# Reordering filter placement, back tables and filler in the prologue of a fused FFT filter and ReGLU kernel

## The chip, the cores and the metric

The kernel runs on one core of a Trainium2 chip. A core has TensorE (PE) for matmuls, VectorE (DVE), ScalarE (ACT) and GpSimd (POOL) for elementwise work, and SyncE (SP), which here only issues DMAs. Each engine runs its instructions in its program order and waits on semaphores of the others. The metric is the device time of one execution in microseconds (us).

## The reference

For x of shape (8, 3008, 256) the reference filters each of the 256 columns along the sequence in the frequency domain, and sends every one of the 24064 resulting rows through a gated feed-forward layer:

```python
X = np.fft.rfft(x, axis=1)
F = (filt_r + 1j * filt_i)[None, :, :]     # (1505, 256)
y = np.fft.irfft(X * F, n=3008, axis=1)    # (8, 3008, 256)

x = y.reshape(24064, 256)
gate = np.maximum(x @ w_gate, 0.0)         # (256, 1536)
val = x @ w_val                            # (256, 1536)
out = (gate * val) @ w_out                 # (1536, 256)
```

## The kernel before

**The transform.** 3008 is 94 x 32, and the transform of a batch is done in two steps by matmuls. `items_a` multiplies x by the table `WA` (94 points) and writes the result to DRAM (`Abuf`); `load_at` reads it back into the tile `at` in another order. Then come six groups i = 0 to 5, in `first_b` for batch 0: `fwd` (line 364) multiplies `at` by the table `F2` (32 points) into two PSUM tiles `psX`, one for each e = 0, 1; `product` (lines 377 to 380) multiplies each `psX` by the filter, `tt` with the real part `Ftr` and `uu` with the imaginary part `Fti`; and `inv` (line 394) multiplies `tt` by the back table `I2t` and `uu` by the back table `I2u`, and adds both in PSUM (`psD`). ScalarE copies `psD` to `dsb`, which goes to DRAM (`Dbuf`) and is read back as `dC`. `item_c` applies the last table `M1` and gives `yT`.

**The layer.** `gv` and `o_part` do the feed-forward layer in 47 blocks of 512 rows, with 12 steps each. The transforms of batches 1 to 7 are placed between these steps at written positions. This steady part begins with the first `item_c`, after the prologue.

**The prologue.** The schedule is manual: on each engine the instructions stand in the order in which the program calls them. The prologue transforms batch 0 and prepares, in this order:

- x is loaded by SP. GpSimd's queue loads the filters (lines 220 and 223: four large loads for `Ftr`, then four for `Fti`; then lines 228 and 231, for each filter a small load of 16 KB into groups 22 and 23 of rows 64 to 95, and one row `nyq`).
- `warm(11)` is filler: matmuls on a constant tile whose result nobody reads (`psJ`, line 511). Then follow the 16 transforms of `items_a(0)`.
- `make_back_t(i)`, three times: matmuls that permute `F2` (line 192), and two VectorE copies into `I2t` (line 197). `make_back_u(i)`, three times: a matmul of `I2t` with a table (line 202), and a ScalarE copy into `I2u` (line 203). After each of the six steps stands `warm(6)`, and one more at the end.
- `place_filter(fi, a, half, copy)` (line 238) copies one half of the 24 groups of a filter (fi 0 is `Ftr`, 1 is `Fti`) from 32 partitions to the next 32; a chooses partitions 0 to 63 or 64 to 127. The four copies for `Ftr` stand between `make_back_t` and `make_back_u`, those for `Fti` behind `place_own` (lines 209 and 211: tables of the last groups, and `M1`). `place_nyq` (line 242) is last.
- Then `first_b(amid)`. Its order on TensorE is fwd 0, filler, fwd 1, filler, fwd 2, inv 0, transforms of batch 1, fwd 3, inv 1, and so on. `amid(0)` and `amid(1)` are filler of 256 columns, the later ones take one or two transforms of `items_a(1)`.

In `product`, a pair (i, e) that is in `POOL_U` has its `uu` made by GpSimd: ScalarE first copies `psX` to `xs` (line 377), since GpSimd reads no PSUM here, and GpSimd multiplies (line 378). All else is made by VectorE (line 380). The two readers of one `psX` follow one another: `xs` is copied when `tt` is done.

## Time and profile before

| | |
|---|---|
| median of 4 runs | 905.04 us (904.13 to 907.09) |
| the profiled execution's own time | 904.13 us |
| its span, first to last instruction | 902.3 us |
| mean granted TensorE clock | 0.993 |
| busy: TensorE, VectorE, ScalarE, GpSimd | 878.6, 568.7, 502.3, 359.4 us |
| first product `psX` of batch 0 on TensorE | starts at 36.22 us |
| first filter product on VectorE | starts at 38.04 us |
| first matmul of the steady part (line 451) | starts at 62.97 us |

All times inside the execution count from the start of the span. A timeline row gives start, length, engine, line, operation, output and inputs and the count, and in brackets how long the engine had been idle before it, and what ended that. A DMA issue row ends with the microseconds from issue to landing. In a table of stretches, the busy time of each engine stands with the number of its instructions, and the last three columns are the granted TensorE clock as a share of full clock, the busy share of the DMA engines, and GB/s. The recorded ends of matmuls are modelled.

### The profile page before, as it was taken

The page shows a single profiled execution, that of the slowest core. Times are in us where ns is not written, and L with a number is a line of the kernel's source. Part 1 is how long each engine was busy: PE and PEld are TensorE (multiplying, and loading weights), DVE is VectorE, ACT ScalarE, POOL GpSimd, SP SyncE. Part 2 cuts the span into 40 slices and gives each one's busy share as a digit, 9 for nine tenths or more (in the row PEclk, how much of TensorE's full clock was granted, in tenths as well). Part 3 has the DMA queues.
Part 4 walks back from the last instruction along what each step waited for, and adds up shares of the span by engine and source line. Part 5 has one row for each costly group of instructions (what it writes and reads, how often), then busy time and mean ns, then how long its engine had stood idle before and what let it go on. Part 6 is the DMA issues. An engine that isn't in the chain of part 4 may idle for free.

```text
span 902.3 us, 19072 instructions
## 1 busy us (share of the span) xinstructions
PE 878.6 (97%) x7089; PEld 511.7 (57%) x7210; DVE 568.7 (63%) x872; ACT 502.3 (56%) x891; POOL 359.4 (40%) x352
## 2 busy tenths in 40 slices
PE   7899999999999999999999999999999999999997
PEld 2335555566555565566655666555655566666664
DVE  2637766577765776667766677657766577655553
ACT  3475565555655555555665565655565555555552
POOL 4232299228670486515773167801868000000000
PEclk9999999999999999999999999999999999999999
DMA  8979358534465344553364433763346512331111
GB/s 233 307 180 192 99 148 192 113 81 112 138 151 123 97 129 124 140 131 109 96 174 122 109 100 104 182 129 85 111 141 148 119 30 82 83 70 36 37 33 50
DMA packets 113759, 109.18 MB, mean 121 GB/s; under 512 B 20290, under 2 KB 98370, under 8 KB 113026
## 3 DMA queue, kind: packets, MB, share of 16 engines
q1 hardware_dynamic: 90662, 80.40, 34.8%
q0 software_dynamic: 22176, 26.01, 12.0%
q10 hardware_dynamic: 828, 1.54, 0.5%
q8 instruction: 57, 0.93, 0.4%
q14 instruction: 36, 0.29, 0.1%
HBM read 61.93 MB, written 49.81 MB: 124 GB/s over the span
## 4 chain that ended last, share of the span: by engine, by line
PE 80%; POOL 5%; DVE 4%; DMA 4%; ACT 4%; issue 3%; SPq 0%; DVEq 0%; POOLq 0%
PE psG L467 24%; PE psO L486 23%; PE psV L467 22%; DVE prod L472 3%; PE psF L323 3%; ACT vsb L470 3%; PE psD L394 2%; PE psA L276 2%; PE psX L364 2%; PE psY L451 1%; DMA WgT<-in_moe_w_gate_dram 1%; DMA XP<-in_x_dram 1%; POOL XP L296 1%; PE psJ L511 1%; DMA XF<-in_x_dram 1%
## 5 line engine op out<-in xcount | busy, mean ns | idle before, releaser
L472 DVE SCALAR_TENSOR_TENSOR prod<-psG,vsb 128x512 bf16<-128x512 f32 x564 | 389.3, 690 | 265.6 <-ACT vsb L470 256.4
L470 ACT CAST vsb<-psV 128x512 bf16<-128x512 f32 x564 | 332.1, 589 | 267.5 <-PE psV L467 203.6
L486 PE MATMUL psO<-WoT,prod 128*128 128x256 bf16 x2256 | 336.5, 273 | 1.1
L467 PE MATMUL psG<-yT,WgT 128*128 128x512 bf16 x1107 | 330.8, 379 | 6.9 <-ACT dsb L401 0.6
L467 PE MATMUL psV<-yT,WvT 128*128 128x512 bf16 x1030 | 315.3, 380 | 1.2 <-ACT yT L456 1.2
L486 PEld LDWEIGHTS <-prod 128*128 128x128 bf16 x2256 | 220.6, 98 | 143.4
L467 PEld LDWEIGHTS <-WgT 128*128 128x128 bf16 x1128 | 109.9, 98 | 136.2 <-issue 2.2
L467 PEld LDWEIGHTS <-WvT 128*128 128x128 bf16 x1128 | 98.4, 98 | 42.3 <-issue 30.9
L258 POOL CAST scr<-yT 128x8 f32<-128x8 bf16 x25 | 4.8, 191 | 266.2 <-ACT yT L456 266.2
L492 ACT COPY osb<-psO 128x512 f32<-128x512 f32 x92 | 54.0, 586 | 27.4 <-PE psO L486 26.3
L380 DVE TENSOR_TENSOR tt<-psX,Ftr 128x512 bf16<-128x512 f32 x96 | 65.1, 683 | 5.1 <-PE psX L364 5.0
L309 POOL TENSOR_TENSOR fold<-XP 128x1024 f32<-128x1024 f32 x24 | 56.6, 2356 | 21.9 <-PE psF L323 20.7
L380 DVE TENSOR_TENSOR uu<-psX,Fti 128x512 bf16<-128x512 f32 x89 | 60.6, 681 | 0.0
L401 ACT CAST dsb<-psD 128x512 bf16<-128x512 f32 x96 | 51.5, 589 | 13.0 <-PE psD L394 12.8
L310 POOL TENSOR_TENSOR XP<-XP 128x1024 f32<-128x1024 f32 x24 | 56.4, 2350 | 1.9
L296 POOL DMA_DIRECT2D XP<-in_x_dram x96 | 56.4, 592 | 0.9 <-issue 0.5
L330 DVE CAST asb<-psF 128x512 bf16<-128x512 f32 x48 | 30.9, 686 | 19.3 <-PE psF L323 15.0
L330 ACT CAST asb<-psF 128x512 bf16<-128x512 f32 x48 | 25.8, 589 | 29.0 <-PE psF L323 29.0
L456 ACT CAST yT<-psY 128x512 bf16<-128x512 f32 x47 | 27.6, 586 | 24.8 <-PE psY L451 24.2
L458 DVE CAST yT<-psY 128x512 bf16<-128x512 f32 x47 | 32.0, 681 | 10.8 <-PE psY L451 10.8
L451 PE MATMUL psY<-M,dC 96*128 96x94 bf16 (+18 forms) x604 | 37.5, 198 | 0.1
L451 PEld LDWEIGHTS <-dC 96*128 96x128 bf16 x604 | 34.5, 97 | 3.5 <-issue 1.2
(66 smaller groups left out, 479.8 us busy)
## 6 DMA issues: line engine op xcount, KB each, us to landing
at<-Abuf SPq DMA_DIRECT2D x32, 384.0 KB
dC<-Dbuf SPq DMA_DIRECT2D x64, 192.0 KB
XP<-in_x_dram POOLq DMA_DIRECT2D x48, 256.0 KB, 6.0
Dbuf<-dsb SPq DMA_DIRECT2D x23, 512.0 KB
XP<-in_x_dram POOLq DMA_DIRECT2D x96, 96.0 KB, 2.7
Abuf<-asb SPq DMA_DIRECT2D x96, 96.0 KB
out_dram<-osb SPq DMA_DIRECT2D x70, 94.0 KB
XF<-in_x_dram SPq DMA_DIRECT2D x15, 256.0 KB
```

Source lines behind the costliest of these rows:

```text
L296: nc.gpsimd.dma_start(xp[r:r + 24, 0:4:2, :], _ap(x, (b * N1 * N2 + o) * D, [[N2 * D, 24], [47 * N2 * D, 2], [1, 512]]))
L309: tt(t, xp[:, 0:2], xp[:, 2:4], op=ALU.add)
L310: tt(xp[:, 2:4], xp[:, 0:2], xp[:, 2:4], op=ALU.subtract)
L330: copy(asf[:, :, q, :], banks[q])
L380: nc.vector.tensor_tensor(p, psX, filt, op=ALU.mult)
L401: nc.scalar.copy(dsb[:, a, o:o + 2, :], psD[a])
L451: nc.tensor.matmul(psY[:, o:o + w], dCs[b, n2 // 8][:, n2 % 8, h * 128:(h + 1) * 128], M1[:, n1:n1 + w], start=True, stop=True)
L467: nc.tensor.matmul(pt[:, :W], w[:, h, ft * 128:(ft + 1) * 128], yt[:, h, :], start=(h == 0), stop=(h == 1))
L470: nc.scalar.copy(vsb, psV[:, :W])
L472: nc.vector.scalar_tensor_tensor(prod, in0=psG[:, :W], scalar=0.0, in1=vsb, op0=ALU.max, op1=ALU.mult)
L486: nc.tensor.matmul(psO[:, t % 2], prods[ft][:, t * 128:(t + 1) * 128], WoT[:, ft, :], start=(ft == 0), stop=(ft == NFT - 1))
L492: copy(osb[:, t0 % 2:t % 2 + 1], psO[:, t0 % 2:t % 2 + 1])
```

## The change

The order of the prologue's preparation is rewritten. The four placements of `Ftr` come first, ahead of the back tables. The three `make_back_t` follow one another, and then the three `make_back_u`, with no filler between them. Of `Fti`, the first placement (a = 0, first half, on VectorE) and the second (a = 1, first half, now on ScalarE) stand ahead of `place_own`, the two of the second half behind it, both on VectorE; before, ScalarE had a = 0 of the second half. All seven `warm(6)` stand at the end. In `POOL_U` the pair (0, 0) is replaced by (1, 0): the first pair has both its products on VectorE, and (1, 0) has its `uu` on GpSimd. `amid(0)` and `amid(1)` issue 5 filler matmuls instead of 3.

```diff
-    POOL_U = ((0, 0), (0, 1), (1, 1), (2, 0), (2, 1), (3, 1), (4, 0))
+    POOL_U = ((0, 1), (1, 0), (1, 1), (2, 0), (2, 1), (3, 1), (4, 0))
...
-    for i in range(3):
-        make_back_t(i)
-        warm(6)
     for half in range(2):
         for a in range(2):
             place_filter(0, a, half, nc.vector.tensor_copy)
     for i in range(3):
+        make_back_t(i)
+    for i in range(3):
         make_back_u(i)
+    place_filter(1, 0, 0, nc.vector.tensor_copy)
+    place_filter(1, 1, 0, nc.scalar.copy)
+    place_own()
+    place_filter(1, 0, 1, nc.vector.tensor_copy)
+    place_filter(1, 1, 1, nc.vector.tensor_copy)
+    place_nyq()
+    for i in range(7):
         warm(6)
-    warm(6)
-    place_own()
-    for half in range(2):
-        for a in range(2):
-            place_filter(1, a, half, nc.vector.tensor_copy if a or not half else nc.scalar.copy)
-    place_nyq()
     load_x(1, nc.sync, ((0, 0, 2 * q), (0, 2 * q, 4 * q), (1, 0, 4 * q)))
 
     early = items_a(1)
 
     def amid(i):
         if i < 2:
-            warm(3, 256)
+            warm(5, 256)
         else:
             for _ in range((1, 1, 2, 1, 1)[i - 2]):
                 next(early)()
```

## The prediction

> **What bounds the kernel now.** I read the page first, then the waits of TensorE, then the timeline of the first 66 us engine by engine, then the DMA issues with their landings, and last the granted clock in stretches of 3.41 us.

> The page's first part: span, then busy time, share and instructions by engine.

> ```profile
> span 902.3 us, 19072 instructions
> PE 878.6 (97%) x7089; PEld 511.7 (57%) x7210; DVE 568.7 (63%) x872; ACT 502.3 (56%) x891; POOL 359.4 (40%) x352
> ```

> TensorE is the bound. The waits of TensorE from 66 us to the end (total, times, longest) start like this:

> ```profile
> PE psG L467 <- ACT dsb L401: 0.6, 1, 0.6
> PE psG L467 <- DVE prod L472: 0.5, 2, 0.3
> PE psG L467 <- DMA WgT<-in_moe_w_gate_dram: 0.4, 1, 0.4
> ```

> Behind the prologue there is almost no wait in which a delay could vanish. So the end moves by what the prologue's last inverse product moves, one for one. Here is the stretch that the change rearranges, from the timeline (start, duration, what, idle before):

> ```profile
> 25.36 0.35 PE L192 MATMUL psI<-tabs,F 64*64 64x64 bf16 x16
> 29.09 0.76 DVE L197 CAST I2t<-psI 128x256 bf16<-128x256 f32 x2 [0.92 <-PE psI L192]
> 29.88 3.87 DVE L238 COPY Ftr<-Ftr 32x3072 bf16<-32x3072 bf16 x4
> 33.54 2.75 PE L511 MATMUL psJ<-junk 128*128 128x512 bf16 x12
> 36.22 0.41 PE L364 MATMUL psX<-at,F 64*64 64x256 bf16 x8
> 38.04 1.89 DVE L380 TENSOR_TENSOR tt<-psX,Ftr 128x512 bf16<-128x512 f32 x3
> 38.77 1.18 ACT L377 COPY xs<-psX 128x512 f32<-128x512 f32 x2 [1.67 <-DVE tt L380]
> 39.44 3.54 POOL L378 TENSOR_TENSOR uu<-xs,Fti 128x512 bf16<-128x512 f32 x3 [2.57 <-ACT xs L377]
> 41.75 0.42 PE L394 MATMUL psD<-uu,I2u 64*64 64x256 bf16 x3 [0.75 <-POOL uu L378]
> ```

> Two things are to be seen. TensorE has no gap from 25.36 to 38.18, because filler lies between the table steps. And its first forward product is ready long before VectorE, which placed filters until 38.01; from 38.18 TensorE mostly waits, until GpSimd's second product ends at 41.71.

> The DMA issue that turns out to decide the change (size, us from issue to landing), and where GpSimd issued it:

> ```profile
> Ftr<-in_filt_r_dram POOLq DMA_DIRECT2D x1, 16.0 KB, 15.1
> 13.34 0.57 POOL L228 DMA_DIRECT2D Ftr<-in_filt_r_dram x1
> ```

> Issued at 13.34, it lands at 13.34 + 15.1 = 28.45. Last the clock (stretch, length, PE busy, ..., the last three PEclk, DMA share, GB/s):

> ```profile
> 9.91:13.32 3.41, 1.06 (x4) 0.23 (x3) 0.00 (x0) 1.16 (x2) 3.41 (x7) 1.00 0.86 243
> 13.32:16.73 3.41, 3.41 (x5) 1.13 (x6) 0.00 (x0) 0.58 (x1) 0.59 (x2) 0.50 1.11 248
> 37.21:40.62 3.41, 1.57 (x23) 0.67 (x16) 3.35 (x8) 1.17 (x2) 1.19 (x2) 1.00 0.98 334
> 40.62:44.04 3.42, 2.66 (x14) 0.91 (x13) 1.70 (x3) 2.04 (x5) 2.23 (x2) 0.50 0.98 317
> 61.10:64.52 3.42, 2.49 (x17) 1.13 (x16) 0.69 (x1) 2.38 (x5) 0.00 (x0) 1.00 0.98 153
> ```

> A stretch with 1.06 or 1.57 us of TensorE work is followed by half clock; 2.49 us is not. The half clock ended after 3.4 us once (13.32) and after 6.8 us once (40.62), where the first stretch held only 2.66 us of work.

> **Part 1: Ftr's four placements go ahead of the back tables.** Each takes 0.95 us (row 29.88). Nothing is added; the order on VectorE changes. The fourth one (second half, rows 64 to 95) reads what line 228 loads, since groups 22 and 23 of those rows are in it. Before, it ran at 32.8 and the load had landed. Now it stands at the head of VectorE's queue at 24.3 and waits for 28.45. Behind it on VectorE are the six copies of the back tables; for them waits TensorE (line 202), and behind that stands all the filler. The first three placements are hidden: their loads have landed by 22.4, where GpSimd's waits for the Ftr loads end. GpSimd's nyq issue at 22.45 shares that moment; even if it slipped by the two copies, 1.9 us, its landing at 28.95 would come before line 242 needs it.

> Worked out: the fourth placement runs 28.5 to 29.45; three pairs of table copies at 0.76 (row 29.09, less overlap) end at 30.2, 30.9 and 31.6; the three matmuls of line 202 follow each pair, the last at 31.65, and filler starts at 31.95. Meanwhile the three steps of line 192, 0.28 each, are done at 26.2. TensorE is idle from 26.2 to 30.25, 4.05 us, then works 0.2 in each 0.7.

> **Part 2: all 42 filler matmuls behind.** Their number stays; six took 1.29 in the chain, so they need 7 x 1.3 = 9.1 us at full clock. In the old order they filled the waits of part 1, and the first forward product started at 36.22. Now that cover is gone. At full clock they end at 31.95 + 9.1 = 41.05. But the idle stretch is emptier than either that lost the clock, so I take half clock. It returns 3.4 to 6.8 us after filler starts, which costs half of that, 1.7 to 3.4. With this trace's 3.41 us grid (the next edges after 33.80 are 37.21 and 40.62) the first full stretch ends at 37.21: 5.26 us at half clock, 2.63 lost. First forward product: 43.68 instead of 36.22, between 41.05 (no loss) and 44.4.

> [...] The trace shows a fall after a gap of only 2.3 us (10.87 to 13.22), so the rows decide.

> **Part 3: Fti's placements, own tables, nyq.** One of the four stays on ScalarE (2.75 us), three on VectorE (0.95 each), own and M1 copies 0.2 each. After 31.6 they need 0.95 + 0.8 + 1.9 + 0.4, so VectorE ends at about 35.6 and ScalarE at 32.8 + 2.75 = 35.55. This is 2.4 us sooner than 38.01, and worth nothing, as the forward product comes at 43.68. The data of that product (at, landed by 34.65) are not last either.

> **Part 4: which product goes to GpSimd.** Seven before, seven after; (0,0) becomes VectorE's, (1,0) GpSimd's. Before, from the first tt to the end of the last product that the first inverse needs: 41.71 - 38.04 = 3.67. After: two tt/uu at the 0.60 pace, tt 0.69, step 0.07, ScalarE's copy 0.59, step 0.08, GpSimd 1.16: 3.79, a loss of 0.12. GpSimd then has four more in a row that the second and third inverse need, 4 x 1.15 = 4.6; ScalarE's copies for them are hidden behind GpSimd. Before, its chain broke at 43.0 to 44.23 and the cold TensorE ended later.

> **Part 5: 5 instead of 3 filler matmuls, twice.** Four more at 0.107 are 0.43 us. They lie in the wait before the first inverse; uncovered they would cost 0.43. TensorE is through its third forward product 2.15 us after its first starts, at 45.8, and then waits for 47.9 with some 0.5 of tt work in it.

> No DMA issue is moved or added on SP, ScalarE or GpSimd; at and the next x keep their clock times, and all that uses them runs later.

> **The sum.** The first product reads its matmul 0.45 after that starts (row pair 47.68, 48.13): 44.13. The first inverse's last operand: 44.13 + 3.79 = 47.92, against 41.71. Does the clock fall there again? The stretch 44.04 to 47.45 holds 1.75 + 0.5 = 2.25 us of work; 1.57 lost it and 2.49 kept it, and 2.25 is nearer to 2.49, so no. Then TensorE is quick and GpSimd is last: 47.92 + 4.6 = 52.5 for the third inverse, whose tail is 0.3; the next transform starts at 52.8 instead of 48.46. That is **+4.3 us**. What follows in the prologue (transforms, Dbuf's way to dC, weights) is released by that chain and moves with it. The profiled execution took 904.13 (span 902.3 and 1.83 around it), the fastest of four; it would be 908.4. Against the median of 905.04: 909.3.

> **The rivals.**

> A, as summed: with the half clock lasting 3.4 to 6.8 us the first forward product lies at 42.75 to 44.4, so 908.3 to 910.1.

> B, the clock falls in the product gap too: the first inverse's tail is at 47.95 instead of 41.75, with the same slow stretch behind it, +6.2: 911.2. For it: a stretch's edges may lie otherwise. Against: the gap of 3.57 becomes 2.1.

> C, the other side: the 16 KB load is not late. If it lands by 24.7, table copies start at 25.73, filler at 28.3, the forward product at 37.4, GpSimd's third-inverse operand at 37.4 + 0.45 + 3.79 + 4.6 = 46.24, the next transform at 46.55 against 48.46: -1.9, 903.1. The point of balance is a forward product at 39.3. That is 12.6 behind the landing at full clock, so a landing at 26.7, or 25.0 with the least clock loss: 1.7 to 3.4 us sooner than shown. For it: the queue's landings can vary. Against: Fti's last large load, ahead of it in the queue, lands at 12.75 + 15.5 = 28.25.

> E, the block comes but TensorE's clock holds: forward product at 41.05, 3.65 later than in C, +1.75: 906.8. Against: two emptier-than-half stretches lost it.

> **How the numbers follow.** A 0.50, B 0.23, C 0.15, E 0.09, still later 0.03. About 0.2% (1.8 us) is what a measurement can tell from no change. C gives most of "faster" (0.11) and the rest of "same" with half of E (0.08); all else is slower (0.81). The range 906.6 to 912.0 holds A, B and E and leaves out C and the late rest; A alone is 908.3 to 910.1.

> **What would show it.** Right: VectorE idle before a line 238 copy until about 28.5, released by Ftr's DMA; TensorE idle near 26 to 30; PEclk 0.5 for 3 to 7 us in the filler; the first line 364 at 43 to 44; VectorE's placements done by 36. Wrong: no DMA wait on VectorE, or the first line 364 before 39.3 (C), filler at full clock (E), or PEclk 0.5 again behind the first inverse (B).

## The result, and the profile after

| | before | after |
|---|---|---|
| median | 905.88 us (60 runs, 901.55 to 910.75) | 909.34 us (39 runs, 905.21 to 917.39) |
| ratio | | 1.0038, 95% interval 1.0027 to 1.0049 |
| profiled execution, its span | 904.13, 902.3 us | 911.06, 909.3 us |
| first forward product, line 364 | 36.22 us | 42.03 us |
| transform behind the third inverse, line 276 | 48.46 us | 51.63 us |
| first matmul of the steady part, line 451 | 62.97 us | 66.14 us |

The changed kernel is slower by 0.38%: 3.5 us by the medians, between 2.4 and 4.4 by the interval. The median forecast was 909.3.

The timeline of the changed kernel, VectorE and TensorE, in the stretch that the change rearranged (start, duration, what, idle before and what ended it):

```profile
22.09 1.92 DVE L238 COPY Ftr<-Ftr 32x3072 bf16<-32x3072 bf16 x2 [4.49 <-DMA Ftr<-in_filt_r_dram]
28.54 0.95 DVE L238 COPY Ftr<-Ftr 32x3072 bf16<-32x3072 bf16 x1 [4.52 <-DMA Ftr<-in_filt_r_dram]
29.52 2.08 DVE L197 CAST I2t<-psI 128x256 bf16<-128x256 f32 x6
...
24.14 0.74 PE L192 MATMUL psI<-tabs,F 64*64 64x64 bf16 x48
30.33 1.91 PE L202 MATMUL psI<-I2t,tabs 128*128 128x512 bf16 x3 [5.45 <-DVE I2t L197]
32.03 0.63 PE L511 MATMUL psJ<-junk 128*128 128x512 bf16 x1
32.89 9.21 PE L511 MATMUL psJ<-junk 128*128 128x512 bf16 x40 [0.22 <-issue]
42.03 0.41 PE L364 MATMUL psX<-at,F 64*64 64x256 bf16 x8
46.27 0.30 PE L394 MATMUL psD<-uu,I2u 64*64 64x256 bf16 x3 [0.94 <-POOL uu L378]
51.63 1.96 PE L276 MATMUL psA<-XF,WA 128*96 128x512 f32 x4
```

Of the two waits on line 238, the first, 4.49 us, is harmless: nothing waits for VectorE yet. The second, 4.52 us, is the fourth placement of Ftr. It starts at 28.54, directly behind the landing of the small load, whose issue row (size, us to landing) in the same trace is:

```profile
Ftr<-in_filt_r_dram POOLq DMA_DIRECT2D x1, 16.0 KB, 15.8
...
12.63 0.57 POOL L228 DMA_DIRECT2D Ftr<-in_filt_r_dram  x1
```

12.63 + 15.8 is 28.43. Behind that placement come the table copies at 29.52, for which TensorE has waited 5.45 us; the filler that used to lie in this wait follows it and ends only at 42.1.

The clock, in stretches of 3.41 us (stretch, length, busy time of PE, PEld, DVE, ACT and POOL with counts; the last three are PEclk, DMA share, GB/s):

```profile
23.47:26.88 3.41, 1.41 (x50) 0.63 (x48) 0.54 (x1) 1.08 (x2) 0.00 (x0) 1.00 1.14 270
26.88:30.30 3.42, 0.00 (x0) 0.00 (x0) 1.73 (x4) 0.00 (x0) 0.00 (x0) 0.50 1.10 342
30.30:33.71 3.41, 3.05 (x6) 0.93 (x8) 3.23 (x9) 2.58 (x4) 0.00 (x0) 0.50 0.67 210
33.71:37.12 3.41, 3.41 (x17) 1.57 (x16) 1.85 (x4) 1.92 (x1) 2.25 (x3) 1.00 1.00 315
43.95:47.36 3.41, 2.12 (x28) 0.95 (x26) 2.80 (x5) 2.33 (x5) 2.29 (x3) 1.00 0.82 146
```

The granted clock fell from 1.00 to 0.50 at 26.88, while TensorE was still idle, and returned at 33.71. So only the first 1.7 us of filler, from 32.03 on, ran at half clock. In the wait before the first inverse (43.95 to 47.36) it held, at 1.00.

Last, the longest waits of TensorE from 66 us to the end (total, times, longest):

```profile
PE psG L467 <- DMA WgT<-in_moe_w_gate_dram: 1.5, 1, 1.5
PE psX L364 <- issue: 1.4, 1, 1.4
PE psV L467 <- ACT yT L456: 1.2, 1, 1.2
```

The first two were 0.4 and 0.4 before; the third also stood in the trace of before, at 64.78, just outside that view. The profiled spans differ by 7.0 us, of which the prologue holds 3.17. By the first output copy (line 492) the difference is 5.27, and behind the ninth it is 6.66. Such waits change from run to run in all kernels of this study: in the nine traces the wait for WgT was between 0 and 1.5 us, that of line 364 between 0 and 1.6. From the ninth to the tenth output copy it took 10.6 to 13.1 us, in no order that follows the edits (10.6 in "old products" below, which has the loss, and 13.1 in "products alone", which has not). From line 451 to the first output copy, however, the two kernels with the loss are the longest: 24.9 us in after and 24.5 in "old products", against 22.7 to 23.6 in the seven others. With one trace of each kernel it stays open whether a part of the loss arises there.

The medians differ by 3.5, close to the prologue's 3.17. But 3.17 compares one pair of executions, and x came 1.2 us earlier in that of after (the table matmuls of line 192 start at 24.14 against 25.36). In after the load is waited for and not x. The order of before follows x: in "products alone" the table matmuls start 0.49 earlier than in before and the first line 364 0.48 earlier. So beside an equally early x the prologue's step would be nearer 4.4 (an estimate: 3.17 + 1.2).

### The profile page after: what moved, and what is told of

It is laid out like the page before. It is cut to its first block, busy times and chain, and to the rows that moved or that the text cites. A ratio compares the mean times of both kernels' runs of the same rounds, so it can differ in the third digit from the quotient of the medians.

```text
span 909.3 us, 19080 instructions
## 1 busy us (share of the span) xinstructions
PE 877.4 (96%) x7094; PEld 511.1 (56%) x7214; DVE 568.7 (63%) x872; ACT 502.1 (55%) x891; POOL 360.4 (40%) x352
## 4 chain that ended last, share of the span: by engine, by line
PE 77%; POOL 5%; DMA 5%; DVE 4%; ACT 4%; issue 4%; SPq 0%; POOLq 0%; DVEq 0%; ACTq 0%
PE psG L467 23%; PE psO L486 23%; PE psV L467 22%; DVE prod L472 3%; ACT vsb L470 3%; PE psF L323 3%; PE psD L394 2%; DMA Ftr<-in_filt_r_dram 2%; PE psX L364 1%; DMA WgT<-in_moe_w_gate_dram 1%; PE psY L451 1%; DMA XP<-in_x_dram 1%; PE psJ L511 1%; POOL XP L296 1%; POOL fold L309 1%
## 5 line engine op out<-in xcount | busy, mean ns | idle before, releaser
L472 DVE SCALAR_TENSOR_TENSOR prod<-psG,vsb 128x512 bf16<-128x512 f32 x564 | 389.3, 690 | 267.0 <-ACT vsb L470 259.0
L467 PE MATMUL psG<-yT,WgT 128*128 128x512 bf16 x1107 | 330.7, 379 | 8.2 <-DMA WgT<-in_moe_w_gate_dram 1.5
L467 PE MATMUL psV<-yT,WvT 128*128 128x512 bf16 x1030 | 315.3, 380 | 1.2 <-ACT yT L456 1.2
L467 PEld LDWEIGHTS <-WgT 128*128 128x128 bf16 x1128 | 109.8, 97 | 137.6 <-issue 2.3
L467 PEld LDWEIGHTS <-WvT 128*128 128x128 bf16 x1128 | 98.4, 98 | 42.3 <-issue 30.9
L380 DVE TENSOR_TENSOR tt<-psX,Ftr 128x512 bf16<-128x512 f32 x96 | 65.1, 683 | 11.6 <-PE psX L364 11.6
L380 DVE TENSOR_TENSOR uu<-psX,Fti 128x512 bf16<-128x512 f32 x89 | 60.6, 681 | 0.0
L401 ACT CAST dsb<-psD 128x512 bf16<-128x512 f32 x96 | 51.5, 589 | 12.1 <-PE psD L394 11.7
L330 DVE CAST asb<-psF 128x512 bf16<-128x512 f32 x48 | 30.9, 686 | 20.5 <-PE psF L323 18.3
L330 ACT CAST asb<-psF 128x512 bf16<-128x512 f32 x48 | 25.8, 589 | 30.4 <-PE psF L323 30.4
```

What stands on the lines that cost most here:

```text
L330: copy(asf[:, :, q, :], banks[q])
L380: nc.vector.tensor_tensor(p, psX, filt, op=ALU.mult)
L401: nc.scalar.copy(dsb[:, a, o:o + 2, :], psD[a])
L467: nc.tensor.matmul(pt[:, :W], w[:, h, ft * 128:(ft + 1) * 128], yt[:, h, :], start=(h == 0), stop=(h == 1))
L472: nc.vector.scalar_tensor_tensor(prod, in0=psG[:, :W], scalar=0.0, in1=vsb, op0=ALU.max, op1=ALU.mult)
```

## The experiments

The theory: the fourth placement of Ftr waits on VectorE for the small load; the table copies, TensorE's table matmuls and all filler stand behind it, and the cover that filler gave is gone. The rivals: the product part costs the time; or filler at the end costs by its place alone; or the load is not what is waited for.

In the table, "tables" is the start of line 192 on TensorE, which depends on when x arrives and differs from run to run; "gap" is from there to the first line 364. The gap shrinks by itself when x comes late and the load is no longer so far behind it, so it is compared with care.

| kernel | tables | line 364 | gap | line 451 | median | ratio to before, 95% interval |
|---|---|---|---|---|---|---|
| before | 25.36 | 36.22 | 10.9 | 62.97 | 905.88 | |
| after | 24.14 | 42.03 | 17.9 | 66.14 | 909.34 | 1.0038 (1.0027 to 1.0049) |
| fourth placement behind | 27.26 | 39.15 | 11.9 | 63.26 | 903.25 | 0.9977 (0.9955 to 0.9998) |
| small load early | 24.97 | 36.98 | 12.0 | 61.09 | 904.81 | 0.9989 (0.9969 to 1.0009) |
| filler between | 25.06 | 37.79 | 12.7 | 63.69 | 904.54 | 0.9993 (0.9970 to 1.0016) |
| old products | 26.37 | 40.69 | 14.3 | 66.94 | 909.48 | 1.0035 (1.0014 to 1.0056) |
| products alone | 24.87 | 35.74 | 10.9 | 61.72 | 905.08 | 0.9998 (0.9971 to 1.0025) |
| early load, 30 filler | 26.95 | 36.43 | 9.5 | 60.54 | 902.99 | 0.9972 (0.9952 to 0.9993) |
| early load, 18 filler | 27.08 | 35.97 | 8.9 | 60.08 | 902.44 | 0.9969 (0.9950 to 0.9988) |

The first four experiments and the last three were run on two different chips. The runs of before beside the first four had a median of 905.92, beside the last three 904.95, so kernels of the two groups are compared by their ratios.

**The fourth placement behind the table copies.** One instruction of the changed kernel moves:

```diff
     for half in range(2):
-        for a in range(2):
+        for a in range(2 - half):
             place_filter(0, a, half, nc.vector.tensor_copy)
     for i in range(3):
         make_back_t(i)
+    place_filter(0, 1, 1, nc.vector.tensor_copy)
     for i in range(3):
         make_back_u(i)
```

> The changed kernel, with only its fourth placement of Ftr (the one that reads the 16 KB load) moved behind the three make_back_t. Theory (the wait for the small load holds VectorE, and with it table copies, TensorE and all filler): the table copies start at about 24.4 instead of 29.5, filler at 27, the first line 364 at about 36.0 instead of 42.0, with no stretch of half clock in the filler; the transform behind the third inverse at about 45.6 instead of 51.6. Time 6 us below the changed kernel and 2.9 below before, about 903.0. Rival 1 (the new GpSimd products or the longer filler behind the first group cost the time): stays at 909. Rival 2 (filler at the end costs by its place, whatever VectorE waits for): line 364 still at 40 or later.

Its timeline, VectorE and then TensorE:

```profile
27.64 2.08 DVE L197 CAST I2t<-psI 128x256 bf16<-128x256 f32 x6 [3.47 <-PE psI L192]
29.75 0.95 DVE L238 COPY Ftr<-Ftr 32x3072 bf16<-32x3072 bf16 x1
...
27.26 0.74 PE L192 MATMUL psI<-tabs,F 64*64 64x64 bf16 x48
28.45 0.39 PE L202 MATMUL psI<-I2t,tabs 128*128 128x512 bf16 x1 [0.45 <-DVE I2t L197]
29.99 9.23 PE L511 MATMUL psJ<-junk 128*128 128x512 bf16 x42
39.15 0.41 PE L364 MATMUL psX<-at,F 64*64 64x256 bf16 x8
```

VectorE now waits for TensorE and no longer for the DMA, and TensorE waits 0.45 us where it waited 5.45. The gap from the tables to the first product is 11.9 us instead of 17.9, but that is no measure of the gain. In this execution x came 3.1 us later than in that of after (27.26 against 24.14), and the small load, though no longer waited for, landed at 13.20 + 14.6 = 27.80:

```profile
Ftr<-in_filt_r_dram POOLq DMA_DIRECT2D x1, 16.0 KB, 14.6
...
13.20 0.59 POOL L228 DMA_DIRECT2D Ftr<-in_filt_r_dram  x1
```

In after the table copies start 1.09 us behind the landing. Here that would have been at 28.9 instead of 27.64, so the wait would have cost this execution only about 1.3 us (an estimate), not the 6 expected. The clock held in the filler (1.00 from 30 to 39). What shows the gain is the median: it is 6.1 us below the changed kernel's (5.5 by the ratios to before), against the 6 expected. With all the filler still at the end and the new products in place, both rivals fall.

**The small load early.** The order on VectorE and TensorE stays; in GpSimd's queue each small load moves ahead:

```diff
     def load_filters():
         for src, dst in FILT:
             for a in range(2):
                 ...
+            nc.gpsimd.dma_start(dst[64:95:2, NG - 2:, :], ...)

     def load_own_filters():
         for src, dst in FILT:
-            nc.gpsimd.dma_start(dst[64:95:2, NG - 2:, :], ...)
             nyq.append(...)
```

> The changed kernel, with its order on VectorE and TensorE untouched, but each 16 KB filter load is issued right behind the four large loads of its own filter, so Ftr's goes ahead of Fti's large ones. Theory: it lands near 23 instead of 28.4, the fourth placement ends near 25.0, the table copies near 27.1, and the first line 364 lies at about 36.6; time 5.4 us below the changed kernel, about 903.6. If the wait is for something other than this load, the fourth placement still starts at 28.5 and the time stays at 909.

```profile
Ftr<-in_filt_r_dram POOLq DMA_DIRECT2D x1, 16.0 KB, 12.2
...
10.65 0.54 POOL L225 DMA_DIRECT2D Ftr<-in_filt_r_dram  x1
...
22.55 2.90 DVE L238 COPY Ftr<-Ftr 32x3072 bf16<-32x3072 bf16 x3 [4.17 <-DMA Ftr<-in_filt_r_dram]
25.48 2.08 DVE L197 CAST I2t<-psI 128x256 bf16<-128x256 f32 x6
```

The load lands at 10.65 + 12.2 = 22.85, and the last three placements run without a break: it was this load. The first product is at 36.98 (expected 36.6), the time 4.5 us below the changed kernel's (expected 5.4).

**Filler between.** Placements stay ahead; filler goes back between the table steps:

```diff
     for i in range(3):
         make_back_t(i)
+        warm(6)
     for i in range(3):
         make_back_u(i)
+        warm(6)
...
-    for i in range(7):
-        warm(6)
+    warm(6)
```

> The changed kernel with its filler put back between the table steps (six matmuls behind each, six more at the end); the placements stay ahead. Theory: VectorE still waits until 28.5 and copies tables at 29.5, but 18 filler matmuls run in that wait, the clock stays full, and the first line 364 lies at about 36.1; time 5.9 us below the changed kernel, about 903.1: the wait costs only where nothing covers it. If the wait itself delays TensorE by 4 us or more whatever lies there, line 364 stays at 40 or later and the time above 907.

```profile
29.11 0.95 DVE L238 COPY Ftr<-Ftr 32x3072 bf16<-32x3072 bf16 x1 [3.73 <-DMA Ftr<-in_filt_r_dram]
30.10 2.08 DVE L197 CAST I2t<-psI 128x256 bf16<-128x256 f32 x6
...
30.58 1.46 PE L511 MATMUL psJ<-junk 128*128 128x512 bf16 x6 [1.80 <-DVE I2t L197]
37.79 0.41 PE L364 MATMUL psX<-at,F 64*64 64x256 bf16 x8
38.83 0.69 DVE L380 TENSOR_TENSOR tt<-psX,Ftr 128x512 bf16<-128x512 f32 x1
```

The wait for the load is still there, 3.73 us. But of it only 1.8 us reach TensorE, and the time is 4.8 us below the changed kernel's. So the wait cost what it did because nothing lay over it. The expectation of 5.9 was 1.1 too high: the load let the placement start 0.6 us later here (29.11 against 28.54), and VectorE was last again. Its first product starts 1.04 us behind the forward product instead of 0.45, because the own tables (line 209) wait for the last line 202 matmul, now at 34.89, and two Fti placements stand behind them until 38.4. In this trace the clock also fell in the wait before the first inverse, to 0.50 for 3.4 us from 42.42.

**The old products on the changed kernel.**

```diff
-    POOL_U = ((0, 1), (1, 0), (1, 1), (2, 0), (2, 1), (3, 1), (4, 0))
+    POOL_U = ((0, 0), (0, 1), (1, 1), (2, 0), (2, 1), (3, 1), (4, 0))
...
-            warm(5, 256)
+            warm(3, 256)
```

> The changed kernel with the old choice of GpSimd's products, (0, 0) instead of (1, 0), and 3 instead of 5 filler matmuls behind the first two groups. Theory: the first line 364 stays at 42.0; the end of the first inverse moves by less than 0.3, the transform behind the third inverse by less than 0.6; time within 0.6 us of the changed kernel, 909.0. Rival (the product part costs the time): near 906. If the shorter filler lets the clock fall behind the first inverse, PEclk shows 0.5 there and the time is about 2 us above the changed kernel.

909.48 against 909.34: the slowdown is there without the product part. In this execution x came at 26.37 and TensorE's wait for the table copies was only 1.66 us; the clock fell in it all the same, to 0.50 from 29.18 to 32.59. The clock also fell in the wait before the first inverse and stayed down for two stretches, from 46.24 to 53.07 (same columns as above; these stretches are set 0.14 us behind the clock's own steps, hence the 0.98):

```profile
42.97:46.38 3.41, 2.10 (x20) 0.75 (x23) 2.44 (x5) 1.67 (x5) 2.97 (x3) 0.98 1.02 284
46.38:49.79 3.41, 3.12 (x27) 1.32 (x26) 1.89 (x3) 2.93 (x7) 2.27 (x2) 0.50 0.31 58
```

That is the prediction's case B, in this one execution; the 2 us above the changed kernel that were expected in that case do not appear in the median, and why is not shown: it may not happen in all executions, or something else makes it good.

**The product part alone on the kernel before** (the same lines the other way round).

> The kernel before with only the product part of the change: (1, 0) instead of (0, 0) on GpSimd, 5 instead of 3 filler matmuls behind the first two groups. Theory: VectorE still places filters until 38.0, the first inverse's last operand comes at 38.04 + 3.79 = 41.8 as before; TensorE works 0.43 more in that wait. Time within 0.5 us of before, 905.9, unless the longer filler keeps the clock full there, which would show as no 0.5 in PEclk behind the first inverse and give up to 1.7 us less. Rival (the product part carries the slowdown): 3 us above before.

905.08 beside runs of before at 904.95: no difference that can be measured. In its execution the clock fell behind the first inverse all the same, to 0.50 for 3.4 us from 42.20. With the experiment above this shows that the product part is not the cause of the loss and gave no gain that the times can tell. The intervals leave room for about 2 us either way, and whether the part makes the fall rarer stays open.

**Less filler, with the small load early.**

```diff
-    for i in range(7):
+    for i in range(5):        # and 3
         warm(6)
```

> The kernel with the 16 KB filter loads issued early, and 30 instead of 42 filler matmuls at the end. Theory (once the wait for the load is gone, the end of the filler sets the first line 364): filler ends 12 x 0.217 = 2.6 us sooner, near 34.4 instead of 37.0, and the data of the first product (at), which landed between 34.4 and 35.9 in the runs so far, are last. Time 1.1 to 2.6 us below the kernel with early loads and 42 matmuls (904.8), so 902.2 to 903.7. Rival (filler is hidden behind at or the filter placements): no change from 904.8.

> The same with 18 filler matmuls. Theory: filler ends near 31.8, TensorE waits for at until 34.4 to 35.9; the first line 364 is where 30 matmuls have it. Time as with 30 if the clock holds over that wait, up to 1.7 us more if it falls. If at were not the limit, 2.6 us less.

```profile
29.81 4.05 PE L511 MATMUL psJ<-junk 128*128 128x512 bf16 x17
35.97 0.41 PE L364 MATMUL psX<-at,F 64*64 64x256 bf16 x8 [2.12 <-DMA at<-Abuf]
```

With 18, TensorE waits 2.12 us for `at`, and the clock held (1.00 from 33 to 37). With 30, the filler ends at 36.32 and the first product starts at 36.43, 0.03 behind GpSimd's read of `at` at 36.40. So in both traces, where x came late (26.95 and 27.08), the data of the first product are the limit once the load is early. Both intervals lie below 1: at 902.99 and 902.44 both kernels are faster than before, by 0.3%, and faster than the changed kernel. Whether they are faster than the kernel with 42 is not clear: the ratios to before (0.9989, 0.9972 and 0.9969) put them 1.5 and 1.8 us below it, as expected, but the intervals overlap. Between 30 and 18 the times tell no difference.

## Why the prediction was right

**The wait.** The fourth placement was forecast at 28.5 and ran at 28.54; the table copies were forecast to end at 31.6 and ended at 31.60. Moving that placement, moving its load or laying filler over the wait took the loss away; putting back the old products did not.

**The filler without cover.** The step "42 matmuls, 9.1 us, behind the wait" was right: 42 of them took 9.23 at full clock where the placement stood behind. Its clock term was over-sized. It took half clock for 5.26 us of filler, until 37.21, a loss of 2.63. The clock returned at 33.71, so that 1.7 us of filler remained, a loss of 0.85, and the first forward product came at 42.03 instead of 43.68. That is earlier than A's own range, 42.75 to 44.4, and later than E's 41.05: A's mechanism was right, with less clock loss than A allows (the sign "PEclk 0.5 for 3 to 7 us in the filler" was 1.7).

What the term had wrong is when the clock returns. The sum gave line 202's three matmuls 0.2 us each and took the first full stretch to be the next one. In the stretch that ended at 33.71 they were busy for 1.80 us at half clock, and with filler the stretch held 3.05; behind it the clock was full. The fall, too, came earlier, at 26.88 instead of about 30.4; TensorE had finished the table matmuls by 24.9 (forecast 26.2). That cost nothing, as TensorE was idle until 30.33.

The fall and the return lie 6.83 us apart, two stretches of 3.41, and the stretch before the fall held 1.41 us of recorded work.

**The products.** From the first tt, 42.48, to the inverse matmul that GpSimd's first product releases, 46.27, are 3.79 us. The forecast of 3.79 was to the end of that product, which lies about 0.05 earlier, so the size was right. The clock held there, as in case A, but the reason given for it does not stand. The forecast put 2.25 us of work in that stretch, and 2.12 came; that they are so close is chance, as the first product was 1.65 us earlier and other work fell into the stretch (0.64 us of the next transform in it). By the rows of before, TensorE is through its third forward product 2.39 us after the first starts (1.96 + 0.43), not 2.15; it took 2.40. And the work recorded in a stretch does not decide: the last section shows stretches of 1.61 us that kept the clock and of 2.03 that lost it. "No fall" was right by luck.

**The third inverse.** It was to follow GpSimd's last product by 0.3. GpSimd's five products ran without a gap and ended at 50.71 (forecast 52.5, less the 1.65 us by which the first product came earlier: 50.85), but the transform came at 51.63, 0.9 later.

```profile
45.07 5.64 POOL L378 TENSOR_TENSOR uu<-xs,Fti 128x512 bf16<-128x512 f32 x5 [8.40 <-ACT xs L377]
48.89 0.30 PE L394 MATMUL psD<-tt,I2t 64*64 64x256 bf16 x2 [0.63 <-ACT xs L377]
50.48 0.41 PE L364 MATMUL psX<-at,F 64*64 64x256 bf16 x8
```

TensorE was itself late by then: the second inverse waited for a PSUM tile until ScalarE's xs copies were done, 0.63 us at 48.89, and the forward product of the fifth group ran only at 50.48. So "ScalarE's copies for them are hidden behind GpSimd" did not hold: this wait was not in the sum.

**The sum.** It was +4.3 at that transform; the traces show +3.17 there, and +3.17 still at line 451. The median moved by 3.5. That the forecast of 909.3 falls so close to 909.34 is luck: it stood on a median of before of 905.04 from four runs, which is 905.88 over sixty, and the forecast step was 0.8 too large. The two errors cancel. A slip in A's range changes nothing here: 42.75 gives 908.5 by the same sum, not 908.3.

**What stayed wrong.** "Behind the prologue there is almost no wait in which a delay could vanish" held, but not that all behind it merely moves along: single waits there vary by 1 to 2 us from run to run, so two profiled spans can differ by twice the effect, and the two kernels with the loss had the longest of them up to the first output copy.

## What to carry to other kernels

Before an instruction is moved ahead on an engine, look up the landing of every load that its source range overlaps, the smallest too: here a 16 KB load issued behind all the large ones landed at 28.43, and the table copies behind it on VectorE, with TensorE idle for 5.45 us, waited for it; issued ahead of Fti's large loads, it landed at 22.85. Filler that lies between dependent steps covers waits that are not there yet: with filler between, 1.80 us of a wait of 3.73 reached TensorE. Moved behind the steps it covers nothing, and a wait that then arises is added to it. Compare two profiled executions at marks near the change, not by their spans, when runs scatter by more than the effect.

## What the runs showed of the hardware

```profile
28.76:32.18 3.42, 1.61 (x9) 0.81 (x9) 3.03 (x7) 0.00 (x0) 0.00 (x0) 1.00 0.84 256
39.00:42.42 3.42, 2.03 (x26) 0.87 (x19) 3.42 (x6) 1.65 (x3) 1.00 (x1) 1.00 1.04 312
...
161.68:165.09 3.41, 3.11 (x37) 0.95 (x35) 1.11 (x2) 0.62 (x3) 1.64 (x2) 1.00 0.30 76
```

The first two rows are of filler between (held, then fell), the third of products alone (fell). In the first TensorE ran mostly 128*128 matmuls, in the second mostly 64*64 ones, and in the third mostly 24*32 ones (line 323). Whether the size of the matmuls plays a part is not shown: no run tried that by itself, and one stretch with 64*64 matmuls held at 2.02 (fourth placement behind).

At half clock it returned behind stretches with 3.05 (after), 3.10 (old products) and 3.21 to 3.42 us, and did not after 2.66 (before) or 3.13 us (old products). The recorded work is a rough measure also because ends of matmuls are modelled. Behind a gap of 2.3 us the clock fell (before, 10.87 to 13.22, 0.50 from 13.32); behind one of 2.12 (early load, 18 filler) it held.

**GpSimd's DMA issues beside VectorE's placements.** In the trace of after the two nyq issues, which start 0.18 and 0.19 us behind a placement, took 0.87 us; before, with VectorE idle, 0.51 and 0.50:

```profile
16.84 0.87 POOL L231 DMA_DIRECT2D nyq<-in_filt_r_dram  x1 [3.64 <-DMA Ftr<-in_filt_r_dram]
18.22 0.51 POOL L228 DMA_DIRECT2D Fti<-in_filt_i_dram  x1 [0.51 <-DMA Ftr<-in_filt_r_dram]
22.28 0.87 POOL L231 DMA_DIRECT2D nyq<-in_filt_i_dram  x1 [3.55 <-DMA Ftr<-in_filt_r_dram]
```

The first four experiments agree: of the 12 nyq issues in their traces and in those of before and after, the 9 that start 0.18 or 0.19 us behind a placement took 0.87 or 0.88 us, and the 3 others, with no placement running, 0.50 or 0.51. In after the first of them ends at 17.71, 0.10 behind the placement's end at 17.61. Why they took longer is not shown: no run changed this alone. Nothing waited for these issues here.
